# Six of eight batches: the second layer taken apart from the first and done by Strassen's seven block products

## The chip, the core and the metric

The kernel runs on one NeuronCore of a Trainium2 chip. A core has five engines with queues of their own, each of which works through its instructions in program order: TensorE (PE; its weight loads are shown as a row of their own, PEld), VectorE (DVE), ScalarE (ACT), GpSimd (POOL) and SyncE (SP), which here issues DMAs. TensorE multiplies a stationary 128x128 block by a moving block of up to 512 columns and adds the product to a PSUM bank; PSUM has eight banks of 512 fp32 columns. The metric is the device time of one execution in microseconds, the median of several.

## The reference

```python
a = softmax(phi, axis=seq)                       # per head: 576 x 32
k_m, v_m = a^T k, a^T v                          # 32 memories of 64 per head
attn = softmax(q k_m^T / 8) v_m                  # 576 x 64 per head
x = attn.transpose(0, 2, 1, 3).reshape(4608, 512)
h = maximum(x @ w_in, 0)                         # 512 -> 2048
out = (h * h) @ w_out                            # 2048 -> 512
```

There are 8 batches of 576 tokens and 8 heads; everything is fp32. (The softmax over `phi` runs over the tokens, and both softmaxes subtract a maximum first.)

## The kernel before

Attention is never formed. For each batch the kernel computes the memories, then `a`, the softmax over 32 memories of each head (256 rows of it in two halves of 128, times the batch's tokens), and `U`, the product of `v_m` and `w_in` (256 x 2048, made in four blocks n of 512 columns). The first layer is then `h = U^T a`. Its operands are split into a high part in TensorE's rounded fp32 format (F32R) and a rest, so that each product takes three matmuls: high x high, low x high, high x low.

Work goes in **steps**. A step takes one tile f of 128 of the 2048 hidden features and one group of tokens. `ffn1` (line 677) does the first layer with six matmuls into a bank `h`, ScalarE takes relu (685), VectorE multiplies relu and `h` to the square (691), ScalarE makes its high part (701), GpSimd or VectorE its low part (705). Two steps later (`LEAD`) `ffn2` (728) multiplies the square by a tile of `w_out` (`wo`, high and low part kept in SBUF) into four accumulating banks, twelve matmuls for four blocks of 128 outputs. The first 56 steps do batches 0 and 1, while weights arrive and are decoded. From batch 2 on the batches go in pairs, and each f of a pair takes three runs of steps: 320 tokens of the first batch, 256 + 256 tokens of both, 320 of the second.

The attention of later batches is work on the side. A table (`early`, `late`) gives for each task the half steps at which its pieces are recorded: `task_phi` and `task_kv` (loads), `task_exp` (213 to 246, on VectorE, its exponential at 244 on ScalarE), `task_mem` (memories: matmuls at 286, scaling and 16 transposes at 303 to 317 on VectorE), `task_u` (a block of U: matmuls at 408, high part 558 on ScalarE, low part 560 on VectorE), and `attend` or `task_both` (scores at 408, softmax at 428 to 468 on VectorE with an exponential at 451 on ScalarE, high part 471 on ScalarE, low part 472 on GpSimd). What is recorded at a place stands there in every engine's queue: an instruction that waits holds up all that is behind it on its engine. `task_stream` brings the decoded `w_in` back from DRAM, a block of 1 MB for each block of U.

Of the kernel before, what the change touches and what calls it, by code (L numbers as in the profile page):

```python
# [24 lines left out]
def attn_moe_kernel(ctx: ExitStack, tc: tile.TileContext, qT, kv, phi, w_in, w_out, outT):  # L25
# [12 lines left out]
    nc = tc.nc  # L38
# [31 lines left out]
    work = ctx.enter_context(tc.tile_pool(name="work", bufs=2))  # L70
    one = ctx.enter_context(tc.tile_pool(name="one", bufs=1))
    dram = ctx.enter_context(tc.tile_pool(name="dram", bufs=1, space=bass.MemoryType.DRAM))
    ps_acc = ctx.enter_context(tc.tile_pool(name="ps_acc", bufs=1, space=PSUM))
    ps_h = ctx.enter_context(tc.tile_pool(name="ps_h", bufs=2, space=PSUM))
    ps_m = ctx.enter_context(tc.tile_pool(name="ps_m", bufs=1, space=PSUM))
# [6 lines left out]

    w_f32 = [dram.tile([P, NPAIR, FC], F32, name=f"w_f32_{n}") for n in range(NFC)]
    HC = w_in.shape[-1] // 2

    def room(f, shape, dtype):
        return const.tile(shape, dtype, name=f"wo{f}")
# [15 lines left out]
    e_sb = const.tile([P, NCH, NQ * P], F32, name="e_sb")  # L103
    kvb = [const.tile([P, 4, CW], F32, name=f"kvb{i}") for i in range(NCH)]
# [13 lines left out]
    ones = const.tile([P, CW - 2 * D], F32, name="ones")  # L118
# [129 lines left out]
    def load_kv(b, qd, lent=None):  # L248

        got = []  # L250
        for c in range(NCH):
            if lent:
# [5 lines left out]
            elif qd:  # L258

                name, bufs = ("tmp", 3) if c < 3 else ("low", 2)  # L260
                if b == 2 and c < 3:
                    if not c:
                        w1 = const.tile([P, 3, 4, CW], F32, name="w1")
                    t = w1[:, c]
                else:
                    t = work.tile([P, 4, CW], F32, name=name, bufs=bufs)
            else:
                t = kvb[c]
                assert c not in kv_used
                kv_used.add(c)  # L270
# [6 lines left out]
        return got  # L277
# [134 lines left out]
    def attend(b, t, q, mem, new_a, u=None):  # L412
# [6 lines left out]
        if u:  # L419
# [105 lines left out]
    def new_a(w):  # L525
        i = a_slots[w].take()
        return (const.tile([P, NQ, w], F32R, name=f"a_hi{i}"), const.tile([P, NQ, w], F32R, name=f"a_lo{i}"), i)

    def new_u():
        i = u_slots.take()  # L530
        if i == 5:
            t = const.tile([P, 2, NQ, FC], F32R, name="w1")
            return t[:, 0], t[:, 1], i
        return (const.tile([P, NQ, FC], F32R, name=f"u_hi{i}"), const.tile([P, NQ, FC], F32R, name=f"u_lo{i}"), i)
# [4 lines left out]
    def new_w(i):  # L539
        return const.tile([P, NPAIR, FC], F32, name=f"w{i}")  # L540

    def stream(n):
        assert n in written
        w = new_w(0)
        nc.sync.dma_start(out=w, in_=w_f32[n])
        return w

    def make_u(b, n, mem, w, got):
# [7 lines left out]
        by_heads([bank(ps, half) for half in range(2)], mem, 1, [w[:, :NQ, n0:n1], w[:, NQ:, n0:n1]])  # L556
# [98 lines left out]
    def split(f, w):  # L655
# [7 lines left out]
    r_room = const.tile([P, 2, WIDE], F32, name="r_room")  # L663
    g_room = const.tile([P, 2, WIDE], F32, name="g_room")
# [70 lines left out]
    def close_all(at, T, acc):  # L735

        o = const.tile([P, NET, T], F32, name=f"o{o_slots[WIDE].take()}")
        ways = ((nc.vector.tensor_copy, nc.sync), (nc.scalar.copy, nc.scalar))
        for e in range(NET):
            parts = [(0, T)] if e < NET - 1 else [(0, T // 2), (T // 2, T)]  # L740
            for i, (x0, x1) in enumerate(parts):
                copy, nc_q = ways[(e + i) % 2 if e < NET - 1 else i]
                copy(o[:, e, x0:x1], acc[e][:, x0:x1])
                nc_q.dma_start(out=outT[e * P:(e + 1) * P, at + x0:at + x1], in_=o[:, e, x0:x1])

    def close(pieces, T, acc, last):
# [3 lines left out]
        if at + T == B * S:  # L750
            close_all(at, T, acc)
            return
# [17 lines left out]
        else:  # L770
# [3 lines left out]
            rooms = [const.tile([P, n, T], F32, name=f"o{i}") for i in got]  # L774
# [23 lines left out]
    def task_kv(b, qd):  # L798
        state[b]["kv"][qd] = load_kv(b, qd)
# [12 lines left out]

    def task_attend(b, t):
        def new():
            state[b]["a"][t] = new_a(width(b, t))
# [5 lines left out]
    streamed = set()  # L821

    def task_stream(b, n):
        w_at[b, n] = stream(n)
        streamed.add((b, n))

    def task_u(b, n, n0=0, n1=FC):
        got = state[b]["u"].setdefault(n, [])
        w = w_at.pop((b, n)) if (b, n) in w_at else w_in_at[n]
        if (b, n) not in streamed:  # L830
# [36 lines left out]
    PER = NT * NFT  # L867
# [16 lines left out]
    def first_kv(qd):  # L884
# [22 lines left out]
    def next_kv():  # L907
        state[1]["kv"][1] = load_kv(1, 1, in_u())
# [58 lines left out]
    for n in kept:  # L967
# [66 lines left out]
        ((112,), task_stream, 2, 3),  # L1034
        ((89, 91), split_out, 2),
        ((89, 90, 91, 91, 91, 94, 96), task_attend, 2, 0),
        ((91,), task_stream, 2, 0),
        ((89,), u_slots.give, 5),
        ((89,), task_q, 2, 1),
        ((105,), task_stream, 2, 2),  # L1040
        ((97,), task_phi, 3),
        ((90,), task_kv, 3, 0),
        ((96,), task_kv, 3, 1),
        ((98,), task_stream, 2, 1),
# [21 lines left out]
    early = [  # L1066
# [164 lines left out]
```

## Time and profile before

| | |
|---|---|
| median of 3 runs | 718.86 us (718.86 to 718.93) |
| span of the profiled execution | 717.0 us |
| TensorE busy | 708.0 us, 5380 matmuls |
| TensorE weight loads | 617.4 us, 5380 loads |
| VectorE, ScalarE, GpSimd busy | 388.6, 332.6, 197.6 us |
| DMA | 89.50 MB, mean 125 GB/s |

The span is the time from the first to the last instruction that the profiler saw; the profiled execution's own time is its 717.0 us and what lies around them. Matmuls overlap in the records, so the time that one takes is read from start to start of a row of them.

### The profile page before, as it was taken

How to read it: one execution, taken by the hardware profiler on the slowest of the kernel's cores; microseconds unless marked ns; L12 is line 12 of the kernel's file. 1: busy time of each engine (PE TensorE's matmuls, PEld its weight loads, DVE VectorE, ACT ScalarE, POOL GpSimd, SP SyncE). 2: the span in 40 equal slices, each digit the busy share in tenths (PEclk: the TensorE clock that was granted, in tenths of full speed). 3: DMA queues.
4: the chain of work that ended last, by engine and by line, in shares of the span. 5: the costliest groups of instructions: out<-in, count | busy, mean ns of one | idle time of the engine just before them, and what ended most of it. 6: DMA issues, size and time to landing. Idle time of an engine off the chain costs nothing.

```text
span 717.0 us, 13710 instructions
## 1 busy us (share of the span) xinstructions
PE 708.0 (99%) x5380; PEld 617.4 (86%) x5380; DVE 388.6 (54%) x835; ACT 332.6 (46%) x644; POOL 197.6 (28%) x221
## 2 busy tenths in 40 slices
PE   9899999999999999999999999999999999999998
PEld 4477798987989998888999999888899899888997
DVE  4978787987686644445472645533573445221211
ACT  2648887875454443323442444323454244332332
POOL 1222103012320133222332334222433243223332
PEclk9999999999999999999999999999999999999999
DMA  9992435331876712083411911146221222100101
GB/s 305 390 351 93 147 138 139 123 122 37 253 243 217 199 59 69 28 230 120 147 59 43 306 69 37 59 145 171 94 89 67 90 96 96 59 1 1 59 1 37
DMA packets 63281, 89.50 MB, mean 125 GB/s; under 512 B 3888, under 2 KB 52272, under 8 KB 59632
## 3 DMA queue, kind: packets, MB, share of 16 engines
q1 hardware_dynamic: 62416, 87.52, 37.9%
q10 hardware_dynamic: 800, 1.10, 0.5%
q8 instruction: 42, 0.69, 0.4%
q14 instruction: 23, 0.19, 0.1%
HBM read 74.97 MB, written 13.63 MB: 124 GB/s over the span
## 4 chain that ended last, share of the span: by engine, by line
PE 93%; DMA 2%; DVE 2%; ACT 1%; issue 0%; POOL 0%; ACTq 0%; SPq 0%; DVEq 0%
PE acc L728 53%; PE h L677 28%; PE ps_m L408 5%; PE acc L720 3%; PE h L286 2%; DMA wo<-in_w_in 1%; DMA u_hi<-in_kv 1%; PE h L408 1%; PE h L149 1%; PE ps_m L350 0%; POOL a_lo L472 0%; DVE at L468 0%; DVE st L465 0%; DVE sm L454 0%; DVE u_lo L560 0%
## 5 line engine op out<-in xcount | busy, mean ns | idle before, releaser
L685 ACT ACTIVATE r_room<-h 128x320 f32<-128x320 f32 (+2 forms) x200 | 95.4, 477 | 262.9 <-PE h L677 256.9
L691 DVE TENSOR_TENSOR g_room<-h,r_room 128x320 f32<-128x320 f32 (+1 forms) x148 | 82.5, 558 | 238.7 <-ACT r_room L685 229.7
L728 PE MATMUL acc<-g_hi,wo 128*128 128x320 f32 (+1 forms) x1024 | 175.5, 308 | 0.0
L728 PEld LDWEIGHTS acc<-g_hi,wo 128*128 128x128 f32 x1024 | 155.6, 188 | 6.1 <-ACT r_room L685 2.5
L705 POOL TENSOR_TENSOR g_lo<-g_room,g_hi 128x320 fp32r<-128x320 f32 (+1 forms) x102 | 89.9, 882 | 223.9 <-DVE g_room L691 166.6
L728 PE MATMUL acc<-o,wo 128*128 128x512 f32 x576 | 139.9, 391 | 0.0
L728 PEld LDWEIGHTS acc<-o,wo 128*128 128x128 f32 x576 | 105.2, 188 | 21.5 <-issue 1.7
L677 PE MATMUL h<-a_hi,u_hi 128*128 128x320 f32 (+1 forms) x448 | 100.9, 306 | 0.7 <-ACT u_hi L558 0.7
L705 POOL TENSOR_TENSOR o<-g_room,o 128x512 fp32r<-128x512 f32 x48 | 62.0, 1291 | 143.7 <-PE acc L728 97.0
L728 PE MATMUL acc<-g_lo,wo 128*128 128x320 f32 (+1 forms) x512 | 100.7, 307 | 0.0
L677 PE MATMUL h<-a_hi,u_lo 128*128 128x320 f32 (+1 forms) x448 | 96.3, 296 | 0.8 <-DVE u_lo L560 0.8
L677 PE MATMUL h<-a_lo,u_hi 128*128 128x320 f32 (+1 forms) x448 | 96.1, 296 | 0.1
L677 PEld LDWEIGHTS h<-a_hi,u_hi 128*128 128x128 f32 x448 | 74.8, 189 | 23.6 <-DVE st L428 9.2
L728 PEld LDWEIGHTS acc<-g_lo,wo 128*128 128x128 f32 x512 | 81.5, 188 | 0.0
L677 PEld LDWEIGHTS h<-a_hi,u_lo 128*128 128x128 f32 x448 | 72.0, 189 | 1.9 <-DVE u_lo L560 1.9
L677 PEld LDWEIGHTS h<-a_lo,u_hi 128*128 128x128 f32 x448 | 72.2, 189 | 0.4 <-POOL a_lo L472 0.4
L701 ACT ACTIVATE g_hi<-r_room 128x320 fp32r<-128x320 f32 (+1 forms) x128 | 59.8, 467 | 7.6
L701 ACT ACTIVATE o<-r_room 128x512 fp32r<-128x512 f32 x48 | 30.4, 633 | 42.4 <-PE acc L728 42.0
L560 DVE TENSOR_TENSOR u_lo<-ps_m,u_hi 128x1024 fp32r<-128x1024 f32 (+1 forms) x29 | 34.3, 1183 | 4.6 <-ACT u_hi L558 4.1
L408 PE MATMUL ps_m<-w,mem 64*32 64x512 f32 (+1 forms) x528 | 35.6, 582 | 0.9 <-POOL w L601 0.9
L720 PE MATMUL acc<-g_hi,wo 128*128 128x256 f32 (+1 forms) x128 | 34.1, 409 | 0.0
L720 PEld LDWEIGHTS acc<-g_hi,wo 128*128 128x128 f32 x128 | 23.2, 190 | 7.0 <-issue 2.0
(175 smaller groups left out, 716.4 us busy)
## 6 DMA issues: line engine op xcount, KB each, us to landing
w<-w_f SPq DMA_DIRECT2D x24, 1024.0 KB, 4.8
wo<-in_w_in SPq DMA_DIRECT2D x16, 512.0 KB, 8.1
wo<-in_w_out SPq DMA_DIRECT2D x16, 512.0 KB, 8.0
kvb<-in_kv SPq DMA_DIRECT2D x28, 256.0 KB, 6.3
q_sb<-in_q SPq DMA_DIRECT2D x16, 320.0 KB, 6.2
out_t<-o SPq DMA_DIRECT2D x30, 160.0 KB, 1.9
e_sb<-in_phi SPq DMA_DIRECT2D x8, 512.0 KB, 6.9
w_f<-w SPq DMA_DIRECT2D x4, 1024.0 KB, 5.7
```

Of the source, the lines that this page charges most:

```text
L149: nc.tensor.matmul(h[:, :k * P], x, ident[:, None, :].broadcast_to([P, k, P]), start=True, stop=True)
L286: nc.tensor.matmul(acc[qd][M * j:M * (j + 1), :CW], e_sb[hs, c, col + M * j:col + M * (j + 1)], kvs[qd][c][hs, j, :], start=(c == 0), stop ...
L408: nc.tensor.matmul(out[half][M * pr:M * (pr + 1), :y.shape[-1]], mem[hs, x, pr], y, start=True, stop=True)
L560: nc.vector.tensor_tensor(out=u_lo[:, :, n0:n1], in0=ps[:, :, :n1 - n0], in1=u_hi[:, :, n0:n1].bitcast(F32), op=ALU.subtract)
L677: nc.tensor.matmul(h[:, at:at + n], u[:, qd, fs], x[:, qd], start=(i == 0), stop=(i == len(todo) - 1))
L685: nc.scalar.activation(r, h[:, :T], AF.Relu)
L691: nc.vector.tensor_tensor(out=g, in0=h[:, :T], in1=r, op=ALU.mult)
L701: nc.scalar.activation(g_hi, r, AF.Square)
L705: adder.tensor_tensor(out=g_lo, in0=g, in1=g_hi.bitcast(F32), op=ALU.subtract)
L720: nc.tensor.matmul(acc[e][:, :T], wo[f][:, e * P:(e + 1) * P], g_hi, start=first, stop=last)
L728: nc.tensor.matmul(acc[e][:, :T], wo[f][:, w, e * P:(e + 1) * P], x, start=first and x is g_hi and w == 0, stop=last and x is g_lo,)
```

## The change

Batches 0 and 1 stay as they are. For batches 2 to 7:

- A step is now one batch and one f: twelve matmuls of 288 columns (two halves of the batch), and one relu of 576 columns, whose result goes to SBUF and, two f at a time (`spill`, 576 KB), to DRAM (`r_f32`, 27 MB in all). Four banks hold two such `h`; nothing of the second layer is between the steps.
- The side work of the next batch (`later`) stands in these 16 steps, 32 half steps. The decoded `w_in` is loaded once and stays. The batch's `kv` loads are spread over half steps 4 to 22.
- When all six batches are through, `second_layer` goes over their 3456 tokens, 384 first and then six blocks of 512. The 384 are done as before, 24 matmuls for a pair of f tiles. In a block of 512 a pair of f tiles, two halves of the tokens and two halves of the outputs make a 2x2 block product, which is done with seven products for eight in seven banks, 42 matmuls of 256 columns. ScalarE squares relu and makes the high part of 1792 columns; VectorE makes the sums of the squares (`combine`), the low part, and the sums of the weights, once for each pair of f tiles (`weights`). At a block's end the seven banks are copied out and added up to the four output blocks (`take_apart`, at the very end `finish_up`).
- The plain `w_out` is stored to DRAM as it is decoded, by 16 DMAs from ScalarE's queue, since `weights` needs it.

```diff
+    def later_a(b, t):
+
+        names = (("a_hi0", "a_lo0"), ("a_hi2", "a_lo2"), ("o1", "o3"), ("r_room", "g_room"))[2 * t + b % 2]
+        return [place([P, NQ, width(b, t)], F32R, name=x) for x in names] + [None]
...
         nc.scalar.copy(wo[f][:, 0], w)
         yield
+        nc.scalar.dma_start(out=w_out_f32[f // 2][:, f % 2], in_=w)
...
-    for b in range(2, B, 2):
-        runs += [(x, 0, NFT) for x in (((b, 0),), ((b, 1), (b + 1, 0)), ((b + 1, 1),))]
...
+    later = [
+        ((2, 3, 5), task_mem, 1),
+        ((3,), task_phi, 2),
+        ((4, 6, 8, 10, 12), task_kv, 2, 0),
+        ((14, 16, 18, 20, 22), task_kv, 2, 1),
+        ((8, 9, 10), task_u, 0, 3),
+        ((9, 10, 11, 12, 13, 14, 15), task_attend, 1, 0),
+        ((10,), task_q, 1, 1),
+        ((16, 17, 18), task_u, 1, 0),
+        ((18, 19, 20, 21, 22, 23, 24), task_attend, 1, 1),
+        ((19,), task_q, 2, 0),
+        ((24, 25, 26), task_u, 1, 1),
+        ((24, 26, 27, 28, 29, 31), task_exp, 2),
+        ((32, 33, 34), task_u, 1, 2),
     ]
...
+    def second_layer():
...
+        def square(i):
+            if i < len(items):
+                n = items[i][1]
+                y[i] = xp.tile([P, 2 * n if n == rest else 8 * HALF], F32, name="y", bufs=3)
+                nc.scalar.activation(y[i][:, :2 * n], raw.pop(i), AF.Square)
+
+        def combine(i):
+            if i < len(items) and items[i][1] != rest:
+                v = y[i].rearrange("p (a n) -> p a n", a=8)
+                for out, in0, in1 in (
+                    (v[:, 4:6], v[:, 0:1].broadcast_to([P, 2, HALF]), v[:, 1:3]),
+                    (v[:, 6], v[:, 2], v[:, 4]),
+                    (v[:, 7], v[:, 3], v[:, 6]),
+                ):
+                    nc.vector.tensor_tensor(out=out, in0=in0, in1=in1, op=ALU.subtract)
...
+        def products(i, acc):
+
+            p = items[i][2]
+            f0, f1 = wo[2 * p], wo[2 * p + 1]
+            for m, of, col, z in (
+                (0, f0, 0, 0), (1, W[p], 2, 5), (2, W[p], 1, 4), (3, W[p], 0, 3),
+                (4, f1, 0, 2), (5, f1, DM // 2, 6), (6, W[p], 3, 1),
+            ):
+                for e in range(2):
+                    for j, (v, u) in enumerate(((0, 0), (1, 0), (0, 1))):
+                        at = col + e * P
+                        w = of[v][:, col, e * P:(e + 1) * P] if of is W[p] else of[:, v, at:at + P]
+                        nc.tensor.matmul(
+                            acc[m][:, e * HALF:(e + 1) * HALF], w, x[i][u][:, z * HALF:(z + 1) * HALF],
+                            start=p == 0 and e == 0 and j == 0, stop=p == NFT // 2 - 1 and e == 1 and j == 2,
+                        )
...
+            load(i + 4)
+            high(i + 1)
+            square(i + 3)
+            if due:
+                next(due)
+            if rest_of:
+                rest_of()
+                rest_of = None
+            combine(i + 2)
+            low(i + 1)
...
+    k = len(steps)
+    for b in range(FUSED, B):
+        for f in range(NFT):
...
+                h = ps_hh.tile([P, 2, 512], F32, name="hh")
+                r = first_layer(b, f, [h[:, t] for t in range(NT)])
+                nc.scalar.activation(r.rearrange("p (t x) -> p t x", t=NT), h[:, :, :S // NT], AF.Relu)
+            half(2 * k)
+            half(2 * k + 1)
+            spill()
+            k += 1
```

The order of instructions shows what this does to the engines, at three places.

TensorE before, from the memories of a later batch on (the start of a run of 320-token steps): `h<-kvb`, `tmp`, `low` are the memories, `ps_m<-w` a block of U, `acc<-g` the second layer of one f, `h<-a` a first-layer step.

```order
L286 MATMUL h<-low,e_sb 32x130 x4
L286 MATMUL h<-kvb_91,e_sb 32x130 x8
L408 MATMUL ps_m<-w_4255,mem 32x512 x8
L728 MATMUL acc_4419<-g_hi,wo_2073 128x320 x2
L728 MATMUL acc_4420<-g_hi,wo_2073 128x320 x2
...
L728 MATMUL acc_4422<-g_lo,wo_2073 128x320
L677 MATMUL h<-a_hi_3880,w_3783 128x320 x4
L677 MATMUL h<-a_lo_3881,w_3783 128x320 x2
```

TensorE after, at the same place of batch 6's memories, in the steps of batch 5: `hh` is a first-layer step, `ps_m<-` a block of U with the new memories, `h<-q_sb,mem` the scores.

```order
L304 MATMUL h<-low,e_sb 32x130 x4
L304 MATMUL h<-kvb_113,e_sb 32x130 x8
L1425 MATMUL hh<-a_hi_3825,u_hi_3851 128x288 x2
L1425 MATMUL hh<-a_hi_3825,u_lo_3852 128x288 x2
...
L1425 MATMUL hh<-g_room,u_hi_3962 128x288 x2
L426 MATMUL ps_m<-u_hi_2625,mem 32x512 x4
L426 MATMUL ps_m<-u_lo_2626,mem 32x512 x4
L426 MATMUL h<-q_sb,mem 32x288 x8
```

Between the memories and the first matmuls that use them there are now three first-layer steps (the rows left out are theirs) and nothing of the second layer; before, second-layer matmuls filled every gap.

VectorE before, from the last steps of `task_exp` to the next scores: `e_sb` is the shifted phi, `u_lo` or `w` the low part of a block of U, `den`, `st` and `mem` the memories, `g_room` a step's square.

```order
L239 TENSOR_TENSOR e_sb<-e_sb,phi_mx 128x256 x4
L241 TENSOR_TENSOR e_sb<-e_sb,phi_mx 64x128 x2
L691 TENSOR_TENSOR g_room<-h,r_room 128x512 x3
L303 TENSOR_SCALAR den<-h 128x1
...
L691 TENSOR_TENSOR g_room<-h,r_room 128x512
L317 STREAM_TRANSPOSE mem<-st 32x2x32 x8
L560 TENSOR_TENSOR u_lo_5347<-ps_m,u_hi_5346 128x1024
L691 TENSOR_TENSOR g_room<-h,r_room 128x512
L317 STREAM_TRANSPOSE mem<-st 32x2x32 x8
L691 TENSOR_TENSOR g_room<-h,r_room 128x512 x3
L428 STREAM_TRANSPOSE st<-h 128x320 x2
```

VectorE after, the same stretch:

```order
L256 TENSOR_TENSOR e_sb<-e_sb,phi_mx 128x256 x4
L258 TENSOR_TENSOR e_sb<-e_sb,phi_mx 64x128 x2
L574 TENSOR_TENSOR u_lo_4530<-ps_m,u_hi_4529 128x1024
L321 TENSOR_SCALAR den<-h 128x1
L322 RECIPROCAL den<-den 128x1
L323 TENSOR_SCALAR st<-h,den 128x2x128
...
L335 STREAM_TRANSPOSE mem<-st 32x2x32 x16
L574 TENSOR_TENSOR u_lo_4670<-ps_m,u_hi_4669 128x1024
L457 STREAM_TRANSPOSE st<-h 128x288 x2
```

The squares are gone. Before, several steps stood between the shift and the scores; now only a block of U stands between the shift and the memories, ahead of them in the queue, and one more between the memories and the scores.

TensorE in the second layer, before, one f of a 512-token run:

```order
L728 MATMUL acc_5034<-o_3169,wo_964 128x512 x2
L728 MATMUL acc_5035<-o_3169,wo_964 128x512 x2
L728 MATMUL acc_5036<-o_3169,wo_964 128x512 x2
L728 MATMUL acc_5037<-o_3169,wo_964 128x512 x2
L728 MATMUL acc_5034<-o_3170,wo_964 128x512
```

and after, in the first block of 512, the first product and a part of the second (`b` is a product's bank, `wo` a tile of weights as it is, `s` sums of weights):

```order
L1293 MATMUL b_6033<-x_hi,wo_1761 128x256 x2
L1293 MATMUL b_6033<-x_lo,wo_1761 128x256
L1293 MATMUL b_6033<-x_hi,wo_1761 128x256 x2
L1293 MATMUL b_6033<-x_lo,wo_1761 128x256
L1293 MATMUL b_6034<-x_hi,s_hi_5801 128x256
L1293 MATMUL b_6034<-x_hi,s_lo_5802 128x256
L1293 MATMUL b_6034<-x_lo,s_hi_5801 128x256
```

Each product is six matmuls of half the width, with a weight load for each.

## Rows read from the trace of the kernel before

**Rows 1.** The page: span, and the engines' shares of the chain that ended last.

```profile
span 717.0 us, 13710 instructions
...
PE 93%; DMA 2%; DVE 2%; ACT 1%; issue 0%; POOL 0%; ACTq 0%; SPq 0%; DVEq 0%
```

**Rows 2.** Windows: each engine's busy us (x instructions), granted clock, DMA share, GB/s.

```profile
217.00:717.00 500.00, 496.54 (x3780) 447.07 (x3778) 218.68 (x479) 190.61 (x355) 153.17 (x161) 1.00 0.30 95
300.00:500.00 200.00, 200.00 (x1602) 176.72 (x1602) 92.28 (x215) 75.03 (x137) 63.82 (x71) 1.00 0.40 120
```

**Rows 3.** Timeline, us 316 to 321, TensorE alone: start, length, engine, line, instructions.

```profile
316.41 0.40 PE L677 MATMUL h<-a_hi,u_hi 128*128 128x256 f32 x2
...
317.00 0.31 PEld L677 LDWEIGHTS h<-a_hi,u_hi 128*128 128x128 f32 x2
...
317.84 2.91 PE L728 MATMUL acc<-o,wo 128*128 128x512 f32 x12
...
320.59 0.40 PE L677 MATMUL h<-a_hi,u_hi 128*128 128x256 f32 x2
```

**Rows 4.** Timeline, two starts of a step of 320 tokens.

```profile
376.69 0.45 PE L677 MATMUL h<-a_hi,u_hi 128*128 128x320 f32 x2
...
379.32 0.45 PE L677 MATMUL h<-a_hi,u_hi 128*128 128x320 f32 x2
```

**Rows 5.** Timeline, one batch's memories, a block of U, VectorE behind them.

```profile
389.95 1.09 PE L286 MATMUL h<-kvb,e_sb 128*32 128x130 f32 x32
...
392.11 1.06 PE L408 MATMUL ps_m<-w,mem 64*32 64x512 f32 x16
392.40 0.16 DVE L303 TENSOR_SCALAR den<-h 128x1 f32<-128x1 f32 x1 [3.07 <-PE h L286]
...
393.10 1.45 PE L728 MATMUL acc<-g_hi,wo 128*128 128x320 f32 x8
...
396.99 1.48 DVE L317 STREAM_TRANSPOSE mem<-st 32x64 f32<-32x64 f32 x8
```

**Rows 6.** VectorE by line and form, us 250 to 660: busy us, mean ns, idle before.

```profile
L560 DVE TENSOR_TENSOR u_lo<-ps_m,u_hi 128x1024 fp32r<-128x1024 f32 x16 | 19.5, 1220 | 1.9 <-ACT u_hi L558 1.5
...
L239 DVE TENSOR_TENSOR e_sb<-e_sb,phi_mx 128x256 f32<-128x256 f32 x16 | 6.1, 441 | 0.1
...
L220 DVE TENSOR_TENSOR phi_mx<-phi_mx,e_sb 128x256 f32<-128x256 f32 x8 | 4.5, 563 | 0.3
...
L443 DVE TENSOR_REDUCE mx<-st 128x20 f32<-128x640 f32 x5 | 4.0, 810 | 0.0
...
L449 DVE TENSOR_TENSOR st<-st,mx 128x512 f32<-128x512 f32 x4 | 2.7, 681 | 0.0
```

**Rows 7.** ScalarE by line and form, us 250 to 660.

```profile
L685 ACT ACTIVATE r_room<-h 128x512 f32<-128x512 f32 x47 | 28.1, 598 | 86.1 <-PE h L677 84.2 <-ACT o L701 1.6
L558 ACT CAST u_hi<-ps_m 128x1024 fp32r<-128x1024 f32 x16 | 16.1, 1004 | 0.2
...
L244 ACT ACTIVATE e_sb<-e_sb 128x1024 f32<-128x1024 f32 x4 | 4.2, 1046 | 0.0
```

**Rows 8.** Timeline, GpSimd beside VectorE.

```profile
335.17 1.29 POOL L705 TENSOR_TENSOR o<-g_room,o 128x512 fp32r<-128x512 f32 x1 [4.65 <-PE acc L728]
...
335.54 1.61 DVE L449 TENSOR_TENSOR st<-st,mx 128x640 f32<-128x640 f32 x1
```

**Rows 9.** Windows, ScalarE: busy us (x instructions), granted clock, DMA share, GB/s.

```profile
120.00:140.00 20.00, 18.65 (x39) 1.00 0.17 57
180.00:200.00 20.00, 8.86 (x21) 1.00 0.96 259
```

**Rows 10.** DMA issues, the page's part 6: KB each, median us to landing.

```profile
kvb<-in_kv SPq DMA_DIRECT2D x28, 256.0 KB, 6.3
```

**Rows 11.** Timeline, the end.

```profile
713.24 0.30 PE L728 MATMUL acc<-g_lo,wo 128*128 128x320 f32 x1
...
714.26 0.34 ACTq L744 DMA_DIRECT2D out_t<-o  x1
```

More of the change, by code (lines that the diff above doesn't have):

```diff
@@ L100, in give @@
             self.free.append(i)
[L103 to L104 removed]
+    e_sb = place([P, NCH, NQ * P], F32, name="e_sb")
+    kvb = [place([P, 4, CW], F32, name=f"kvb{i}") for i in range(NCH)]
     def fill(c, t):
@@ L539, in new_w @@
     def new_w(i):
[L540 to L546, printed above, removed]
+        return place([P, NPAIR, FC], F32, name=f"w{i}")
     def make_u(b, n, mem, w, got):
@@ L555, in make_u @@
         ps = new_ps(True)
-        by_heads([bank(ps, half) for half in range(2)], mem, 1, [w[:, :NQ, n0:n1], w[:, NQ:, n0:n1]])
+        by_heads([bank(ps, half) for half in range(2)], mem, 1, [x[:, :, n0:n1] for x in w])
         yield
@@ L798, in task_kv @@
     def task_kv(b, qd):
-        state[b]["kv"][qd] = load_kv(b, qd)
+        if b > FUSED + 1:
+            return load_kv(b, qd)
+        for _ in load_kv(b, qd):
+            pass
     def task_exp(b):
@@ L907, in next_kv @@
     def next_kv():
-        state[1]["kv"][1] = load_kv(1, 1, in_u())
+        for _ in load_kv(1, 1, in_u()):
+            pass
     loads = [
@@ L1108, in attn_moe_kernel @@
+    for b in range(FUSED, B):
+        for places, fn, x, *args in later:
+            if b + x < B:
+                at([begin + STEP * (b - FUSED) + p for p in places], fn, b + x, *args)
     queue = []
@@ new lines, in attn_moe_kernel, with spill, first_layer @@
+    pairs = [None] * 2
+    spills = []
+    def spill():
+        while spills:
+            b, f, r = spills.pop()
+            s0 = (b - FUSED) * S
+            nc.sync.dma_start(out=r_f32[f // 2][:, :, s0:s0 + S], in_=r)
+    def first_layer(b, f, banks):
+        n = f * P // FC
+        fs = slice(f * P % FC, f * P % FC + P)
+        u_hi, u_lo, slot = state[b]["u"][n][0]
+        T = width(b, 0)
+        for t in range(NT):
+            assert ("u", b, f * P) in ready and ("a", b, t) in ready, (b, t, f)
+            a_hi, a_lo, _ = state[b]["a"][t]
+            todo = [(u, x, qd) for u, x in ((u_hi, a_hi), (u_lo, a_hi), (u_hi, a_lo)) for qd in range(NQ)]
+            for i, (u, x, qd) in enumerate(todo):
+                nc.tensor.matmul(
+                    banks[t][:, :T], u[:, qd, fs], x[:, qd], start=(i == 0), stop=(i == len(todo) - 1)
+                )
+        if f % 2 == 0:
+            pairs[0] = place([P, 2, S], F32, name=f"o{f % 4}")
+        r = pairs[0][:, f % 2]
+        if f % 2:
+            spills.append((b, f, pairs[0]))
+        if f * P % FC + P == FC:
+            u_slots.give(slot)
+        return r
@@ new lines, in attn_moe_kernel @@
+    k = len(steps)
+    for b in range(FUSED, B):
+        for f in range(NFT):
+            if k < len(steps) + LEAD:
+                banks = [ps_h.tile([P, 512], F32, name="h") for _ in range(NT)]
+                r = first_layer(b, f, banks)
+                for t in range(NT):
+                    nc.scalar.activation(r[:, t * S // NT:(t + 1) * S // NT], banks[t][:, :S // NT], AF.Relu)
+                if queue:
+                    finish(queue.pop(0))
+                if k == len(steps) + LEAD - 1:
+                    assert not queue
+                    sums.close()
+                    ps_hh = sums.enter_context(
+                        tc.tile_pool(name="ps_hh", bufs=2, space=PSUM, reuse_waits="tile")
+                    )
+            else:
+                h = ps_hh.tile([P, 2, 512], F32, name="hh")
[5 more added lines that the diff above has]
+            k += 1
+            if b == B - 1 and f == CLOSE:
+                assert not under_way
+                attention.close()
+                second = second_layer()
+            if b == B - 1 and f in AHEAD:
+                next(second)
@@ L1199 @@
+    next(second, None)
 def kernel(q, k, v, phi, moe_w_in, moe_w_out):
```

317 lines of the change are left out of this document (219 added, 98 removed).

## The prediction

> **What bounds the kernel now.** I read the chain that ended last first: TensorE holds 93% of it, no other engine more than 2% [rows 1]. [...] So time comes off only where TensorE has less to do, and every wait that the change gives TensorE is lost in full. The last view is the timeline, for what a matmul costs from start to start.
>
> **The price of a matmul.** Twelve of 256 columns start at 316.41 and end where twelve of 512 start, 317.84: 1.43 us, 119 ns each. The twelve of 512 reach to 320.59: 2.75 us, 229 ns each [rows 3]. A step of eighteen of 320 columns takes 379.32 - 376.69 = 2.63 us, 146 ns each [rows 4]. These lie on one line of 0.43 ns a column, so I put 288 columns at 133 and 384 at 174 ns (estimates between rows).
>
> **First layer.** For each f and pair of batches, 12 x 119 + 12 x 146 = 3.18 us before and 24 x 133 = 3.19 us after. Nothing.
>
> **Second layer.** Before, 24 x 146 + 12 x 229 = 6.25 us for an f and pair, 48 times: 300.1 us. After, the 384 tokens take 8 x 24 matmuls at 174 ns, 33.4 us, and the six blocks 6 x 8 x 42 = 2016 matmuls at 119 ns, 239.9 us; together 273.3. The gain is 26.8 us. It rests on short matmuls keeping their 119 ns when 336 of them follow each other, each with a weight load of its own. The row of a load stands beside the matmuls, 317.00 inside 316.41 to 317.84, and TensorE doesn't pause for it [rows 3]. [...]
>
> **The side work, closer together.** A batch's first-layer stage takes TensorE 16 x 12 x 133 ns = 25.6 us, and the next batch's side work 4 blocks of U at 1.0 (392.11 to 393.10), memories 2.2 (389.95 to 392.11) [rows 5], two scores at about 0.55 (half a block of U, as an estimate): 32.9 us. Before, the same side work was spread over half a pair, 16 x 9.43 / 2 + 7.3 = 83 us. VectorE has to do in it: low parts of U 4 x 1.22; for phi some 7.3 (three maxima at 0.56, four shifts at 0.44, and small passes); two attentions of 576 columns, each a half transpose twice and five passes between 0.68 and 0.81, about 5.1 with the small ones [rows 6]; memories 1.6 from 392.40 and two groups of eight transposes at 1.5 [rows 5], 4.6. That makes 27 us, 82% of the stage. ScalarE: 16 relus at 0.66 (0.60 for 512 columns), U 4.0, phi 1.3, attention 2.8, so 19 us [rows 7]. No engine is over-full, so order decides. Set 0 at the end of the second scores (place 18). TensorE has six f tiles and a block of U, 10.6, then two tiles of the next batch and a block of U: at 14.8 it comes to the memories. VectorE needs 6.2 for the attention (with ScalarE's exponential and hand-overs), 1.9 for the maxima, 1.2 for a block of U, 2.9 and 2.3 for the rest of phi: 14.5. I add 0.8, since GpSimd's low part of `a` falls on the maxima: a VectorE pass of 640 columns that takes 0.81 [rows 6] took 1.61 beside a GpSimd pass [rows 8]. ScalarE's exponential ends at 16.6, so TensorE waits 1.8. Memories end at 18.8. VectorE's next row is not theirs but the block of U, which waits for ScalarE's relu and high part, 18.3, and ends at 19.5; then 4.6 and hand-overs, 24.5. TensorE has three tiles to do, to 23.6, and waits 0.9 for the block of U that needs the new memories. Late next is the first attention, but its TensorE work is behind the same wait and the two are level again by the second scores. So 2.7 us a batch, for the memories of batches 4 to 7: 11 us. Bounds: 0, if hand-overs are short, and 32, 8 us a batch with most of them exposed. I take the walked value.
>
> **DMAs of that stage.** Spills 4.7 MB, kv 2.4, q 1.2, phi 0.6: 8.9 MB in about 35 us, 253 GB/s. At 259 GB/s the share was already 0.96 [rows 9]. From half step 4 to 22 it is some 6.2 MB in 19 us, 326 GB/s. A buffer of two tiles is written again three tiles, 4.8 us, after it was closed, and TensorE lacks a bank 1.6 us later; a kv load among others took 6.3 us to land [rows 10]. I take nothing, with 0 to 3 us a batch as bounds: all these DMAs stand in SP's one queue, but kv pieces are between spills, not ahead of them.
>
> **Smaller terms.** Batches 0 and 1: 16 DMA issues on ScalarE's queue at 0.34 us (the issue at 714.26 [rows 11]), 5.4 us, where ScalarE is 18.65 of 20 busy at one place and 8.86 at another [rows 9]; I take 2, bounds 0 and 6. PSUM changes hands twice: before the first `hh`, VectorE empties the four accumulators beside the memories' matmuls; before the second layer the last relu must be done. 2, bounds 0 and 4. Within a block an item takes 42 x 119 = 5.0 us; ScalarE needs 1.05 for the square and some 1.7 for the high part, VectorE 0.68 + 2 x 0.44 for the sums and about 2.0 for the low part (extended from [rows 6, 7]). The high part can start with the item before, the low part is ready at 3.8: covered by 1.2 us. Block ends add four copies and eight sums to VectorE, spread over five items: 1, bounds 0 and 6. Weight sums come to 3 us in eight items: covered. The end: from the last matmul at 713.24 it is 3.8 us to the end of the span [rows 1, 11]; the last addition and a store of 256 KB make it 1 longer, 0 to 2.
>
> **Sum.** The profiled execution's span is 717.0 us [rows 1], with 1.9 around it, which makes the median of 718.86. 718.9 - 26.8 + 11 + 2 + 2 + 1 + 1 = 709.1.
>
> **Rivals.** (1) All of it is covered, since VectorE and ScalarE have free time in the sum; only the end and a hand-over cost: 718.9 - 26.8 + 2 = 694, up to 700. For it speaks the 18% that VectorE has free; against it the queue order, in which memories wait behind a block of U. Chance 0.22. (2) Slower: VectorE's chain sets the pace of the first-layer stage. If each hand-over is exposed (attention's exponential 1.5 twice, phi's exponential, relu and memories 4.2, four blocks of U 2.7 each with their relu), 18 us come to VectorE's 27: 45 for 32.9, five stages, 60 us, 752. It decides from 5 us a stage on, 20.8 / 4, a stage of 38 us; between, with 6 to 9 a stage, 721 to 733. Speaks for it that TensorE's gaps were filled by second-layer work that is gone; against, that half of these hand-overs lie beside other rows. Chance 0.13. (3) Spills land late and relu, then TensorE, wait, 2 to 3 us in five stages: 715 to 722, chance 0.11. (4) The short matmuls don't hold 119 ns: at 132 the gain is gone, at 146, what 320 columns take, 54 us are lost: 764. The rows speak against it; 0.03. The forecast, 702 to 715, has 0.51.
>
> **The numbers.** No change is anything within 0.2%, 717.4 to 720.3, about what a measurement of this kernel can tell. Faster: forecast, (1) and half of (3), 0.78. Same: 0.06, from (3) and the upper end. Slower: (2), (4) and the rest of (3), 0.16. The range 695 to 722 leaves out the lowest part of (1) and most of (2) and (4).
>
> **What the profile after would show.** Second layer: 42 matmuls in 5.0 us without idle time, about 275 us from the first `b` to the last. First-layer stages of 35 to 36 us; TensorE waiting at the memories for ScalarE's exponential, and at the first block of U behind them for VectorE's transposes, some 2 and 1 us, in four batches; none in batch 7's stage. Relu waits for TensorE, not for a DMA. The prediction is wrong if a 256-column matmul's row is 130 ns or more, if a stage stays at 33 or passes 38 us, if relu waits for spills, or if the granted clock falls below 1.00 at a wait.

## The result and the profile after

The changed kernel takes 707.97 us in the median (706.97 to 708.43), 718.86 before: a ratio of 0.9847, with a 95% interval of 0.9833 to 0.9861. The prediction's sum was 709.1, its range 695 to 722. The span fell from 717.0 [rows 1] to 706.2 us, by 10.8.

The page after: span, busy time, and the engines' shares of the chain that ended last.

```profile
span 706.2 us, 14494 instructions
...
PE 686.6 (97%) x5860; PEld 612.8 (87%) x5860; DVE 531.6 (75%) x967; ACT 395.8 (56%) x575; POOL 59.1 (8%) x86
...
PE 76%; DVE 12%; DMA 4%; ACT 4%; issue 2%; SPq 0%; POOL 0%; ACTq 0%; DVEq 0%
```

TensorE holds 76% of the chain for 93%: where it was full for 200 of 200 us [rows 2], it now has gaps. The windows say where. I cut them at the first matmuls of batches 2 to 7, of the 384 tokens and of the six blocks. Columns: length, busy us (x instructions) of PE, PEld, DVE, ACT and POOL, granted clock, DMA share, GB/s.

```profile
213.46:252.69 39.23, 38.19 (x394) 32.32 (x393) 26.84 (x62) 17.10 (x27) 3.80 (x7) 1.00 0.70 221
252.69:289.56 36.87, 34.89 (x370) 28.78 (x369) 26.59 (x66) 17.17 (x26) 3.07 (x6) 1.00 0.76 241
...
326.40:363.22 36.82, 34.80 (x370) 28.77 (x369) 26.60 (x66) 17.25 (x26) 3.07 (x6) 1.00 0.77 242
363.22:399.16 35.94, 34.53 (x371) 28.82 (x370) 24.09 (x61) 17.48 (x26) 2.85 (x2) 1.00 0.42 150
399.16:427.13 27.97, 27.97 (x227) 25.95 (x226) 3.32 (x3) 14.59 (x21) 0.00 (x0) 1.00 0.57 199
427.13:460.62 33.49, 33.49 (x194) 33.25 (x193) 23.74 (x40) 20.40 (x23) 0.00 (x0) 1.00 0.80 272
460.62:700.73 240.11, 239.68 (x2016) 239.27 (x2016) 205.06 (x260) 135.51 (x116) 0.00 (x0) 1.00 0.42 125
```

The second layer has hardly a gap (239.68 us busy of 240.11): 33.49 + 240.11 = 273.6 us, 240.11 / 2016 = 119 ns a matmul with its load. What TensorE loses, it loses in the first-layer stages, 36.8 us for 35 to 36. Its waits, over the whole program (us in total, times, longest); before it had none of either kind:

```profile
PE h L304 <- ACT e_sb L261: 5.0, 4, 1.3
PE hh L1425 <- ACT o L1456: 3.2, 9, 0.8
```

The first is the foreseen one. TensorE's timeline at one batch's memories:

```profile
330.25 0.42 PE L1425 MATMUL hh<-r_room,u_lo 128*128 128x288 f32 x2
330.51 0.43 PE L1425 MATMUL hh<-g_room,u_hi 128*128 128x288 f32 x2
332.20 1.09 PE L304 MATMUL h<-kvb,e_sb 128*32 128x130 f32 x32 [1.26 <-ACT e_sb L261]
...
334.50 0.53 PE L1425 MATMUL hh<-a_hi,u_hi 128*128 128x288 f32 x2
334.87 0.42 PE L1425 MATMUL hh<-a_hi,u_lo 128*128 128x288 f32 x2
```

It waits 1.26 us for ScalarE's exponential of phi. The rows also show something smaller: two matmuls of 288 columns take 0.26 us from start to start (330.25 to 330.51), but 0.37 right behind side work (334.50 to 334.87).

VectorE's timeline ahead of that exponential shows why it is late:

```profile
322.82 2.15 DVE L237 TENSOR_TENSOR phi_mx<-phi_mx,e_sb 128x256 f32<-128x256 f32 x2
...
325.64 1.23 DVE L574 TENSOR_TENSOR u_lo<-ps_m,u_hi 128x1024 fp32r<-128x1024 f32 x1
...
330.98 0.58 DVE L258 TENSOR_TENSOR e_sb<-e_sb,phi_mx 64x128 f32<-64x128 f32 x2
```

No row in this stretch has idle time ahead of it; a block of U (325.64) stands in the middle, and two maxima take 2.15 us where one took 0.56 before [rows 6].

The second wait was not in the forecast. ScalarE's timeline near the end of the same stage:

```profile
358.68 0.65 ACT L1456 ACTIVATE o<-hh 128x576 f32<-128x576 f32 x1 [1.81 <-DMA r_f<-o]
359.34 0.67 ACT L491 CAST o<-at 128x576 fp32r<-128x576 f32 x1
359.92 1.01 ACT L572 CAST u_hi<-ps_m 128x1024 fp32r<-128x1024 f32 x1
360.83 1.27 ACT L1456 ACTIVATE o<-hh 128x576 f32<-128x576 f32 x2
```

Relu waits 1.81 us for the spill that last read its buffer, the two casts behind it are late, and so is the next relu: TensorE lacks a bank twice. In us 213 to 425 relu waits for spills ten times:

```profile
ACT o L1456 <- DMA r_f<-o: 18.0, 10, 2.6
```

The DMA view of us 336 to 360 (share in 40 slices, then the sum, then the spills issued there with their median time from issue to landing):

```profile
DMA  5999999999999999999999999999999999985995
...
DMA packets 8108, 7.61 MB, mean 317 GB/s; under 512 B 365, under 2 KB 6594, under 8 KB 8105
...
r_f<-o SPq DMA_DIRECT2D x6, 576.0 KB, 5.5
```

The DMA engines are full for nearly all of this stretch, and a spill takes 5.5 us in it.

The timeline at the end:

```profile
700.73 0.28 PE L1293 MATMUL b<-x_lo,s_hi 128*128 128x256 f32 x1
...
700.84 2.17 SPq L1304 DMA_DIRECT2D out_t<-m  x4
701.33 1.28 DVE L1310 TENSOR_TENSOR m<-b,m 128x512 f32<-128x512 f32 x2
```

From the last matmul to the end of the span it is 5.5 us, 3.8 before [rows 1, 11].

### The profile page after: what moved, and what is told of

The parts are those of the page before. It is cut to its first block, busy times and chain, and to the rows that moved or that the text cites. A ratio compares the mean times of both kernels' runs of the same rounds, so it can differ in the third digit from the quotient of the medians.

```text
span 706.2 us, 14494 instructions
## 1 busy us (share of the span) xinstructions
PE 686.6 (97%) x5860; PEld 612.8 (87%) x5860; DVE 531.6 (75%) x967; ACT 395.8 (56%) x575; POOL 59.1 (8%) x86
## 4 chain that ended last, share of the span: by engine, by line
PE 76%; DVE 12%; DMA 4%; ACT 4%; issue 2%; SPq 0%; POOL 0%; ACTq 0%; DVEq 0%
PE b L1293 33%; PE hh L1425 11%; PE acc L743 10%; PE h L692 7%; PE b L1276 5%; PE acc L735 3%; PE ps_m L426 3%; PE h L304 2%; DMA r_f<-o 2%; DMA wo<-in_w_in 1%; DVE phi_mx L237 1%; DMA u_hi<-in_kv 1%; DVE at L488 1%; DVE st L485 1%; DVE sm L474 1%
## 5 line engine op out<-in xcount | busy, mean ns | idle before, releaser
L1227 DVE TENSOR_TENSOR x_lo<-y,x_hi 128x1792 fp32r<-128x1792 f32 (+1 forms) x56 | 104.7, 1870 | 49.7 <-ACT x_hi L1223 49.7
L1223 ACT CAST x_hi<-y 128x1792 fp32r<-128x1792 f32 (+1 forms) x56 | 87.9, 1570 | 96.2 <-PE b L1293 52.1
L1293 PE MATMUL b<-x_lo,s_hi 128*128 128x256 f32 x384 | 108.1, 281 | 0.0
L1293 PE MATMUL b<-x_hi,wo 128*128 128x256 f32 x576 | 107.9, 283 | 0.0
L1293 PE MATMUL b<-x_hi,s_hi 128*128 128x256 f32 x384 | 107.9, 281 | 0.0
L1293 PE MATMUL b<-x_hi,s_lo 128*128 128x256 f32 x384 | 107.9, 281 | 0.0
L1293 PEld LDWEIGHTS b<-x_hi,wo 128*128 128x128 f32 x576 | 89.9, 192 | 0.0
L1293 PE MATMUL b<-x_lo,wo 128*128 128x256 f32 x288 | 81.5, 283 | 0.4 <-DVE x_lo L1227 0.3
L1216 DVE TENSOR_TENSOR y<-y 128x512 f32<-128x512 f32 x144 | 73.7, 512 | 3.4
L743 PE MATMUL acc<-g_hi,wo 128*128 128x320 f32 (+1 forms) x256 | 43.2, 301 | 0.0
L700 ACT ACTIVATE r_room<-h 128x320 f32<-128x320 f32 (+2 forms) x56 | 24.7, 441 | 27.5 <-PE h L692 26.6
```

The source lines that it names most:

```text
L700: nc.scalar.activation(r, h[:, :T], AF.Relu)
L743: nc.tensor.matmul(acc[e][:, :T], wo[f][:, w, e * P:(e + 1) * P], x, start=first and x is g_hi and w == 0, stop=last and x is g_lo,)
L1216: nc.vector.tensor_tensor(out=out, in0=in0, in1=in1, op=ALU.subtract)
L1223: nc.scalar.copy(x[i][0], y[i])
L1227: nc.vector.tensor_tensor(out=x[i][1], in0=y.pop(i), in1=x[i][0].bitcast(F32), op=ALU.subtract)
L1293: nc.tensor.matmul(acc[m][:, e * HALF:(e + 1) * HALF], w, x[i][u][:, z * HALF:(z + 1) * HALF], start=p == 0 and e == 0 and j == 0, stop=p ...
```

## The experiments

The theory is that of the prediction, corrected by the trace: the second layer gains by columns, and more than half is given back, much of it because the side work, closer together, makes relu and the exponential of phi late. Three questions follow: is the gain Strassen's, what makes TensorE wait, and are the two ends worth mending. Each run is compared with the kernel before (718.98 to 719.11 us on the chips used).

**Plain second layer.** Each block is done as the 384 tokens are, in four banks, by 24 matmuls of 512 columns for a pair of f tiles:

```diff
-                products(i, acc)
+                plain(i, acc)
```

> The six blocks of 512 tokens are done as the 384 are, 24 matmuls of 512 columns for a pair of f tiles (output unchanged); no sums of squares or weights. Theory (a matmul costs 0.43 ns a column plus some 9 ns, and its weight load is hidden at 256 columns): an item takes 24 x 229 ns = 5.5 us for 5.0, 48 items 24 us more, less 1 to 2 at the end, so 729 to 732 us, slower than before the change by 10 to 13. Rival (the short matmuls pay for their weight loads, so that seven products gain little over eight): within 8 us of the changed kernel, 700 to 716.

Measured: 725.69 us, 1.0104 of before (1.0090 to 1.0117). The windows of the 384 tokens and of the six blocks:

```profile
425.27:458.70 33.43, 33.43 (x195) 33.39 (x194) 8.11 (x9) 16.39 (x21) 0.00 (x0) 1.00 0.52 163
458.70:719.50 260.80, 260.80 (x1153) 215.90 (x1151) 57.59 (x47) 105.70 (x117) 0.00 (x0) 1.00 0.37 112
```

The seven products are worth 260.80 - 240.11 = 20.7 us in the layer and 17.7 in the median. Without them the separation of the layers is a loss of 6.7 us. The size missed the expectation by 3 to 6 us: a matmul of 512 columns takes 260.80 / 1152 = 226 ns here for the 229 of a row of twelve (3 us), and the second layer begins 1.9 us sooner in this execution (425.27 for 427.13). From the last matmul to the end it is 4.0 us, 1.5 less than with the seven products, as expected.

**The scores first.** The second scores of a batch go ahead of a block of U:

```diff
-        ((16, 17, 18), task_u, 1, 0),
+        ((19, 20, 21), task_u, 1, 0),
-        ((18, 19, 20, 21, 22, 23, 24), task_attend, 1, 1),
+        ((16, 17, 18, 20, 21, 22, 23), task_attend, 1, 1),
```

> The second scores of a batch and their softmax stand two half steps ahead of the block of U that they followed. Theory (VectorE's queue from these scores to the exponential of phi is full, and it idled 2 us ahead of that block's low part): the waits of 1.3 us at the memories of four batches go, 5 us, so 702 to 704 us. Rival (VectorE is slowed where GpSimd computes beside it, and the rest of the stage sets the pace): the wait moves to another row of the same stage, 707 to 709.

Measured: 705.51 us, ratio 0.9811 (0.9798 to 0.9824), 2.5 less than the changed kernel, between theory and rival. Both of the waits above are gone from TensorE's list, and a new one stands at its head:

```profile
PE ps_m L426 <- DVE u_lo L574: 7.0, 5, 1.4
```

ScalarE's timeline gives the cause: the exponential of the softmax (L471) stands behind a relu that waits for TensorE.

```profile
315.23 0.65 ACT L1456 ACTIVATE o<-hh 128x576 f32<-128x576 f32 x1 [1.72 <-PE hh L1425]
315.77 0.68 ACT L471 ACTIVATE st<-st 128x576 f32<-128x576 f32 x1
```

On VectorE the next row of the softmax, the sum at 316.49, has 2.31 us of idle time ahead of it, and the low part of U behind it is late by as much.

**The exponential sooner.** The exponential goes ahead of that relu, the rest one place up:

```diff
-        ((16, 17, 18, 20, 21, 22, 23), task_attend, 1, 1),
+        ((16, 17, 18, 19, 20, 21, 22), task_attend, 1, 1),
```

> As the run with the scores first, but the exponential of that softmax stands at place 19, ahead of the next relu, and what follows it one place earlier. There ScalarE's exponential waited behind a relu that waited for TensorE, VectorE lost 2 us, and TensorE waited 1.4 us for the low part of U, five times. Theory (the order in ScalarE's queue is what is left of the stall): these 7 us go and none comes in their place, 698 to 700 us. Rival (VectorE is full between these places whatever the order): the wait moves again, 703 to 706.

Measured: 703.23 us, ratio 0.9784 (0.9770 to 0.9797). The rival's range: VectorE's 2 us are won, but the low part of U still stands behind the softmax, and the wait only shrinks.

```profile
PE ps_m L426 <- DVE u_lo L574: 5.3, 5, 1.3
...
PE hh L1425 <- ACT o L1456: 0.4, 1, 0.4
```

TensorE hardly waits for relu here, though relu itself still waits for the spills (us 213 to 425):

```profile
ACT o L1456 <- DMA r_f<-o: 14.4, 9, 2.4
```

**Spills one by one.** A spill is 288 KB and goes to `r_f32[f // 2][:, f % 2]`:

```diff
-        if f % 2:
-            spills.append((b, f, pairs[0]))
+        spills.append((b, f, r))
```

> Each f is spilled by a DMA of its own (288 KB) as soon as its relu is done; buffers as they were. Theory (relu waits for the spill of two f tiles that used its buffer, and TensorE then for relu, 4 us in all): half of the bytes leave 1.6 us earlier, most of these waits go, 704 to 706 us. Rival (ScalarE is late because the high part of U stands between two relus): 707 to 708.5. Rival (twice the DMA issues hold up the kv loads behind them): 709 to 711.

Measured: 705.83 us, ratio 0.9815 (0.9802 to 0.9828): 2.1 us less than the changed kernel, as expected. The wait:

```profile
PE hh L1425 <- ACT o L1455: 2.2, 6, 0.8
```

Relu's wait falls from 3.2 to 2.2 us, not away. Whether the spills are its cause was still open.

**Half of the spilled bytes.** Relu is as long as before, but only its first 288 tokens are spilled (`r_f32` has half the columns), and the second layer reads those for the others too; no other work changes.

```diff
-            nc.sync.dma_start(out=r_f32[f // 2][:, :, s0:s0 + S], in_=r)
+            nc.sync.dma_start(out=r_f32[f // 2][:, :, s0:s0 + S // 2], in_=r[:, :, :S // 2])
```

> The changed kernel, but only the first 288 of 576 tokens of each relu are spilled, and the second layer reads those in the place of the others: half of the spilled bytes, the same instructions. Theory (relu waits because the DMAs of kv, q and spills together fill the DMA engines): TensorE's waits for relu, 3.2 us in nine, fall under 0.5, about 704.5 us. Rival (ScalarE's queue order): they stay at 3 us, 707 to 708.5.

Measured: 703.59 us, ratio 0.9787 (0.9771 to 0.9803), 4.4 us less than the changed kernel. The waits:

```profile
PE h L304 <- ACT e_sb L261: 5.0, 4, 1.3
...
PE hh L1425 <- ACT o L1456: 0.8, 4, 0.3
```

and relu's own, in us 213 to 425:

```profile
ACT o L1456 <- DMA r_f<-o: 6.6, 6, 1.6
```

The wait for the exponential is untouched, that for relu falls from 3.2 to 0.8, and relu's own for the spills from 18.0 to 6.6. So the second one comes from the DMAs, as theory has it. But ScalarE's order has a part in it: with the exponential sooner relu waited 14.4 us for spills, and TensorE for relu only 0.4. Either edit takes most of TensorE's wait away. It is 2.4 of the 4.4 us; the profiled execution is 5.5 us shorter, 3.7 of them in the first-layer stages, the rest ahead of batch 2 and in the second layer.

**The two ends.**

```diff
-        nc.scalar.dma_start(out=w_out_f32[f // 2][:, f % 2], in_=w)
+        nc.sync.dma_start(out=w_out_f32[f // 2][:, f % 2], in_=w)
...
-            add(m[3], m[3], m[2])
+            nc.gpsimd.tensor_tensor(out=m[3], in0=m[3], in1=m[2], op=ALU.add)
...
-            add(m[6], acc[6], m[1])
-            store(t0, 0, 0, m[6])
+            for e, q in ((0, nc.scalar), (1, nc.sync)):
+                c = slice(e * HALF, (e + 1) * HALF)
+                add(m[6][:, c], acc[6][:, c], m[1][:, c])
+                t = FUSED * S + t0
+                q.dma_start(out=outT[e * P:(e + 1) * P, t:t + HALF], in_=m[6][:, c])
```

> Two edits at the two ends of the program: the 16 stores of w_out are issued by SyncE and no longer by ScalarE, and the last block's end has one sum on GpSimd and its last store in two halves on two queues. Theory: the first matmul of batch 2 comes at 212.7 for 213.5, and from the last matmul to the end it is 4.2 for 5.5 us, so 705.5 to 706.5 us. Rival (the early 0.8 us are the bytes of these stores and not their issues, and SyncE's queue holds loads behind them): the first matmul of batch 2 stays or is later, 706.5 to 709.

Measured: 715.65 us, ratio 0.9957 (0.9942 to 0.9973), 7.7 us more than the changed kernel. The rival was right and far too small: the first matmul of batch 2 comes at 222.97 for 213.46. On SyncE's queue five of these stores take 9.44 us, with the loads of q behind them:

```profile
161.81 9.44 SPq L674 DMA_DIRECT2D w_out_f<-tmp  x5
171.30 0.97 SPq L415 DMA_DIRECT2D q_sb<-in_q  x2
```

The profiled execution is the slowest of the six, 718.82 us, and its clock is a part of that. Ahead of us 177.5 TensorE had waited 1.6 and 0.3 us close together, ahead of 215.1 it had waited 1.5 and 0.4, and behind both its granted clock fell below 1.00; in the changed kernel it is 1.00 all the way to 213 us.

```profile
172.00:200.00 28.00, 26.10 (x217) 21.88 (x216) 18.67 (x57) 14.34 (x30) 6.11 (x8) 0.94 0.57 161
200.00:223.00 23.00, 21.10 (x156) 17.09 (x155) 14.94 (x32) 10.31 (x21) 6.57 (x9) 0.93 0.91 298
```

An estimated 28 x 0.06 + 23 x 0.07 = 3.3 of the 9.5 us are the clock's, about as much as this execution lies above the median, and 5.7 are TensorE's waits from us 120 on, where the changed kernel has none. Which of the loads behind the stores each wait goes back to was not followed.

On ScalarE's queue nothing is behind these stores that TensorE needs soon: in the plain run, whose first 213 us are the same, batch 2 begins at 212.67, at 212.65 before. The end is 5.58 us and not shorter: it is not one store that is late, but 1 MB.

**All three together.** The sooner order, single spills, and an end in which the first output is stored after the fourth product:

```diff
+            early = xp.tile([P, 2 * HALF], F32, name="raw")
+            add(early, m[3], m[2])
+            store(t0, 1, 0, early)
+            nc.gpsimd.tensor_tensor(out=m[1], in0=m[1], in1=m[3], op=ALU.add)
-            add(m[1], m[1], m[3])
...
-            add(m[3], m[3], m[2])
-            store(t0, 1, 0, m[3])
```

> The order of the run with the exponential sooner, one spill for each f, and the last block's sums in another order (the first output is stored after the fourth product, one sum on GpSimd). If the three add up: 699 less 2 for relu's waits, less 1 at the end (from the last matmul to the end 4.4 for 5.5 us): 696 to 698. Rival (the sooner order already has relu off the spills, and the end is bound by 1 MB of stores): 698 to 700.

Measured: 700.55 us, ratio 0.9743 (0.9727 to 0.9758). That is above both ranges, because the sum set out from 699 and the sooner order alone takes 703.23; from there the two other edits give 2.7 us, about the 3 expected of them. The end is 4.77 us. Its DMA view, us 693 to 699:

```profile
DMA  0000000004999999999999999999981000000000
...
DMA packets 1088, 1.05 MB, mean 175 GB/s; under 512 B 64, under 2 KB 1088, under 8 KB 1088
```

Once the stores have begun, they fill the DMA engines until all is stored; beginning sooner is what helped.

**The second block of U later.**

```diff
-        ((24, 25, 26), task_u, 1, 1),
+        ((26, 27, 28), task_u, 1, 1),
```

> The best order, with the second block of U of the stage two half steps later. Theory (TensorE there waits up to 0.9 us for the low part of the block before, in four or five batches, 2.3 us): the waits go, about 698 us. Rival (they come back at the memories, since VectorE's low part now stands ahead of the subtractions of phi): 700 to 701.

Measured: 699.59 us, ratio 0.9726 (0.9709 to 0.9744). The interval overlaps with that of the run before, so 1 us is not certain, but the wait for the low part of U, 2.3 us there, is 0.2, and none came back at the memories.

```profile
PE ps_m L426 <- DVE u_lo L574: 0.2, 1, 0.2
```

**The low part of `a` on VectorE.**

```diff
-        (nc.vector if starting else nc.gpsimd).tensor_tensor(out=a_lo, in0=at, in1=a_hi.bitcast(F32), op=ALU.subtract)
+        (nc.vector if starting or b > FUSED else nc.gpsimd).tensor_tensor(out=a_lo, in0=at, in1=a_hi.bitcast(F32), op=ALU.subtract)
```

> The changed kernel, but the low part of a (one pass of 576 columns, twice a batch, batches 3 to 7) is made by VectorE and no longer by GpSimd. Theory (the maxima of phi on VectorE, 1.07 us each, are slowed by GpSimd's pass beside them): they take 0.56, VectorE's queue is 0.3 shorter though it has a pass of 0.7 more, and TensorE's wait at the memories falls from 1.25 to about 0.9 us in four batches: 706.5 us. Rival (their time is their own): 1.07 stays, the wait grows to 1.9, 710.5 us.

Measured: 709.16 us, ratio 0.9857 (0.9842 to 0.9873). By line and form, first of the changed kernel:

```profile
L237 DVE TENSOR_TENSOR phi_mx<-phi_mx,e_sb 128x256 f32<-128x256 f32 x12 | 11.4, 946 | 0.4
```

and of this run:

```profile
L237 DVE TENSOR_TENSOR phi_mx<-phi_mx,e_sb 128x256 f32<-128x256 f32 x12 | 6.3, 525 | 0.4
L492 DVE TENSOR_TENSOR a_lo<-at,a_hi 128x576 fp32r<-128x576 f32 x5 | 3.8, 759 | 3.7 <-ACT a_hi L491 3.7
```

The mechanism is right, the maxima fall from 946 to 525 ns. The balance is not: VectorE's pass costs 759 ns and it waits 0.7 us ahead of each for ScalarE's high part. The wait at the memories grows from 5.0 to 6.1 us. The time lies 1.2 us above the changed kernel's, with overlapping intervals.

The same edit on the best order:

> As the one before, with the low part of a on VectorE in batches 3 to 7. If GpSimd's pass slows VectorE by as much as VectorE's own pass costs: the same as the one before within 1 us; if not, VectorE's queue is 1.4 us a batch longer and the wait at the memories returns: 2 to 4 us more.

Measured: 700.79 us, ratio 0.9744 (0.9730 to 0.9757), 1.2 more than without it; overlapping intervals, no gain.

**Short matmuls.** Appended to the changed kernel, for the price of a product with a load of its own:

```diff
+                for w in (256, 192, 128, 64):
+                    bank = ps.tile([P, 512], F32, name="b7")
+                    for j in range(96):
+                        nc.tensor.matmul(
+                            bank[:, :w], wo[j % NFT][:, j // NFT % 2, :P], x[i][0][:, :w],
+                            start=j == 0, stop=j == 95,
+                        )
```

> Behind the changed kernel's last product 4 x 96 matmuls with a weight load each follow, of 256, 192, 128 and 64 columns, into the free bank. Theory (a matmul costs 9 ns and 0.43 ns a column, the load is hidden): 119, 92, 64 and 37 ns from start to start. Rival (a load of 128 columns is hidden only as long as it is the shorter one): the time stops falling at some width, and all widths below cost the same; if that floor is near 110 ns, 256 columns is about the shortest product that pays.

Measured, from one profiled execution: windows from the first to the last start of each width (TensorE's busy time, granted clock, DMA share, GB/s).

```profile
701.38:712.78 11.40, 11.40 (x97) 1.00 0.28 93
713.12:723.81 10.69, 10.69 (x96) 1.00 0.00 0
724.14:734.80 10.66, 10.66 (x95) 1.00 0.01 2
735.14:752.54 17.40, 17.40 (x95) 0.59 0.00 1
```

There are 95 spacings in each: 120, 113, 112 and 183 ns for 256, 192, 128 and 64 columns. The rival is right: from 192 columns down the time stays at 112 to 113 ns, as long as the clock is 1.00. That the load sets it is argued and not shown, as each of these matmuls has one. (The 64 columns also hold it at first, 111 to 112 ns, until the clock falls; see the last section.)

## Why the prediction was right, point by point

**Matmuls: -26.8 forecast, -26.5 with the same price before.** 300.1 [rows 3, 4] less 273.6. An item took 240.11 / 48 = 5.0 us as forecast. The plain run splits it: about 6 us come from wider matmuls (300.1 to 294.2), 20.7 from seven products for eight. The rival of short matmuls is excluded, but closer than it looked: the straight line of 0.43 ns a column, which I took for all widths, ends at 112 ns, and 256 columns stand 7 ns above that. The loads lie beside the matmuls, their rows busy for 239.27 of the six blocks' 240.11 us.

**Side work: +11 forecast, as 1.8 + 0.9 us in four batches.** The total nearly came out (15.7 us were given back, 2.8 of them by the smaller terms below), its parts did not. The wait at the memories was there, in four batches and for ScalarE's exponential: 5.0 us for 7.2. The 0.9 us behind them were not: the block of U behind the memories is the running batch's and doesn't read the new memories; I took it for the next one's, in the section on the change too. In its place came 3.2 us of relu's waits, which I had put at nothing. By spans, these two, 0.8 at the start, 0.3 at the first blocks and 1.7 at the end give -26.5 + 11.0 = -15.5, where -10.8 was measured. The other 4.7 us are in no wait that the views name.

**First layer: nothing forecast, 6.9 measured.** Here those 4.7 us show. I added up TensorE's time from the start of each matmul to the start of the next, idle time left out, from batch 2 on. The 1152 first-layer matmuls take 161.7 us for 154.8 before, the side work 39.8 for 38.5, the second layer (with 24 matmuls left over from the first 56 steps) 277.3 for 307.3: +6.9 + 1.2 - 30.0 = -21.9 in place of -26.5. One cause is what the rows at the memories showed. Behind side work the first two matmuls of 288 columns start 0.24 us apart for 0.13, and the last one ahead of it takes 0.23. Some 30 runs of first-layer steps now stand between side work, where 22 runs of either layer did; the prediction priced no such border. Another is that at twelve of TensorE's waits the matmul ahead takes 0.29 us for 0.13 before idle time is counted. By these counts the two make an estimated 1.6 and 1.9 of the 4.7 us. No run tests this.

**VectorE's chain.** VectorE's and ScalarE's loads were read nearly rightly, 26.6 and 17.2 us in a stage for 27 and 19. That GpSimd would slow the maxima was right: 0.8 us forecast, 2 x (1.07 - 0.56) = 1.0 measured, and the run without GpSimd's pass confirms it, 525 ns for 946 in the mean of the twelve. (The prediction's 0.81 us is the row of another operation, L443; the line that took 1.61, L449, takes 0.82 in three of its five passes of 640 columns, so the reading holds.) That order and not load decides was right too: three changes of the table (scores first, exponential sooner, U later) took no work away, and with them and the single spills TensorE's waits for the exponential and for the low part of U are down to 0.2 us.

**Spills: nothing forecast, up to 3 a batch as bound.** Mis-sized. The step "kv pieces are between spills, not ahead of them" looked at the queue's order, not at the engines' share. They were nearly full for 24 us, and a spill took 5.5 us there, longer than the 4.8 us that its buffer allows. Relu waiting for spills is one of the prediction's own signs of being wrong, and that sign appeared. Rival (3) was at work, at a quarter to a third of its 2 to 3 us in five stages (which on top of 709.1 are 719 to 724, and not 715 to 722): TensorE waited 3.2 us for relu, and half the bytes gave back 4.4 us. (Rival (2), which did not come about, has 721 to 733 where its terms give 722 to 734.) The other signs did not appear: 119 ns a matmul, stages of 36 to 37 us, a granted clock of 1.00 at the waits. (The first stage's 39.2 us hold 3.7 us of the second layer of batches 0 and 1.)

**Smaller terms.** DMA issues on ScalarE: 2 forecast, 0.8 in this execution and nothing in the plain run with the same instructions; over all runs with them batch 2 begins at 212.3 to 214.0, so 0.8 is no more than scatter. PSUM hand-overs: 2 forecast; the second layer's first matmul follows 0.14 us after the last first-layer one, so nothing. Block ends: 1 forecast, none found in 240.11 us. The end: 1 forecast, 1.7 measured, since I counted one store where four compete. The smaller terms, 6 in all, make 2.8 with the waits at the first blocks.

So the mechanism and the size of the gain were read rightly; that the price came to within 1 us is in part errors that cancel: too much on the order and on the hand-overs, nothing on the spills and on the first layer's matmuls.

## What to carry to other kernels

Taking two interleaved stages apart removes what filled the gaps of the one: first count what the side work needs on every engine and on the DMAs in the shorter stage, then walk its order queue by queue, since here another order, smaller spills and a sooner first store took a further 8 us off, to 699.59. Fewer products for more additions paid here with matmuls of 256 columns, 119 ns each; with a weight load each they hardly got cheaper below that, 112 ns at 128 columns. Count the places where matmuls meet side work: each cost TensorE some 0.2 us here without a wait that a view names. Where DMA buffers turn round quickly, compare the share of the DMA engines in that stretch with 1.00, not the mean over the stage (here 36 of 40 slices of us 336 to 360 were at 90% or more, 0.77 over the stage).

## What the runs showed of the hardware

A matmul with a load of its own took 113, 112 and 111 to 112 ns from start to start at 192, 128 and 64 columns while the granted clock was 1.00; at 256 it took 119 to 120. And with 64 columns the clock was taken back although TensorE had hardly paused. The windows of that stretch, TensorE alone (granted clock, DMA share, GB/s):

```profile
736.00:738.00 2.00, 2.00 (x20) 1.00 0.00 0
738.00:740.00 2.00, 2.00 (x14) 0.58 0.00 0
740.00:742.00 2.00, 2.00 (x11) 0.50 0.03 8
```

Ahead of it stood 96 matmuls of 128 columns and some 28 of 64, each with a load, with no gap but 0.06 us where the width changes; then the granted clock went from 1.00 to 0.50, and a matmul took 213 ns for 112. Products of 256 columns held 1.00 for all of 240 us.
